# Signs of the input weights on VectorE, a transposed block copy, and redrawn planner priorities in a fused delta-rule and two-layer-pair kernel

## The chip, the cores and the metric

The kernel runs on one core of one Trainium2 chip. The metric is device time in microseconds; the median of three runs of the kernel before is 1029.02 us (1028.18 to 1032.16). In the profile PE is TensorE's matmuls, PEld its weight loads, DVE VectorE, ACT ScalarE, POOL GpSimd and SP the engine whose queue issues the DMAs.

## The reference

Three steps follow each other. The first is a delta-rule recurrence over 768 steps for 4 batches and 8 heads of width 48; its output, reshaped to 3072 tokens of 384 features, goes through two layer pairs with 2048 hidden features each.

```python
for t in range(S):
    kt, vt, bt = (k_n[:, :, t], v[:, :, t], beta[:, :, t, None])
    y[:, :, t] = np.einsum('bhd,bhde->bhe', q[:, :, t], state)
    v_old = np.einsum('bhde,bhd->bhe', state, kt)
    state = state + bt[:, :, :, None] * np.einsum('bhd,bhe->bhde', kt, vt - v_old)
...
h = x @ w_in;  g = np.where(h > 0, h, np.exp(np.minimum(h, 0)) - 1);  x = g @ w_out
...
h = x @ w_in
P = a[0] + a[1] * h + a[2] * h**2 + a[3] * h**3
Q = 1.0 + np.abs(b[0]) * np.abs(h) + np.abs(b[1]) * h**2
out = (P / (Q + 1e-06)) @ w_out
```

The weights of the layer pairs are double precision and reach the kernel as pairs of 32-bit words.

## The kernel before, in words

**Recurrence.** The 768 steps are cut into 12 chunks of 64, and two chunks make a window (six windows). For each window the Gram products of `g_in` (tiles `gp`, `gd`) are turned into small triangular systems, 32 to a partition, and `t_pieces` (lines 792 to 876) inverts their unit triangular matrices in tile `tt`: seven `row` steps for blocks of 8, eight for blocks of 16, then the off-diagonal block by two products, `px` (four steps: `tt` by `am` into `xx_t`) and `pt` (four steps: `xx_t` by the lower right block of `tt` into `tt`), and `post`, which scales a block and transposes all into `tp_t`. Each step is one product and one sum over the last axis on DVE (`step`, line 833). Then `chain` (line 901) runs each chunk: `ks`, a solve in three parts (`cb`), `yy`, `ku`, which renews the state `s_bd`, and `xx`, the transposition into `xs`. Chunks depend on each other through `s_bd`.

**Layer pairs.** All matrix products of the layer pairs are done in three passes with operands split into a high and a low part (`xh` and `xl`, `gh` and `gl`, two halves of `wi` and of `wor` or `wo`). One block of 9 matmuls of 512 columns makes a hidden tile (`h`) or adds a hidden tile to the output (`o`). The first pair runs window by window, 16 hidden tiles each, with the recurrence of the next window between its blocks. The second pair runs afterwards, 48 steps of 18 and 18 matmuls.

**Weight conversion.** A double-precision word pair becomes a float in `conv_x`, `conv_d` and `conv_s` (lines 657 to 697), in halves of 192 columns: two ACT passes scale the high and the low word; DVE joins them by a shift and an or; then the sign has to be put in. For the second pair (`i2`, `o2`) a second DVE operation takes it from the high word by an and with the top bit. For the first pair (`i1`, `o1`) ACT computes the sign of the high word and POOL multiplies. The first pair's input weights, `i1`, are 16 tiles of two halves, 32 conversions; they pass through tile `ce` and are split into `wi` by an ACT copy and a POOL subtraction. Most of their raw words lie in a part of `wo1` (tile name `wo`) that is free at that time.

**Order.** No engine's order is written by hand. Every operation is recorded with its costs, and `order` (line 311) simulates the machine for eight rounds: an engine takes, of what is ready, the operation with the earliest latest start (`late`), TensorE the group with the smallest number; `backward` (line 530) works out new latest starts from the round before, less a random amount of up to `jit` ns. The best round's order is issued. `SLACK` (line 308) holds its margins, among them the time by which a wide group counts as ready late (`F`). In the head, where TensorE would idle, `gaps` (line 338) puts in filler matmuls (`fill`), as many as the planned idle time holds.

The six windows' `tt` lie in one buffer, `ce` in two; SP issues loads of raw words a few conversions ahead, from within `conv_d`.

Of the kernel before, what the change touches and what calls it, by code (L numbers as in the profile page):

```python
# [10 lines left out]
F32 = mybir.dt.float32  # L11
# [3 lines left out]
AF = mybir.ActivationFunctionType  # L15
# [147 lines left out]


class Op:
    __slots__ = ("n", "eng", "emit", "deps", "succ", "pitch", "lat", "group", "key", "start", "late", "off", "left", "ready", "bytes", "tag", "port")


class Group:
    __slots__ = ("kind", "ops", "n")  # L170


class Recorder:
# [133 lines left out]
SIZE = {"F": 9, "yy": 16, "yt": 48}  # L307
SLACK = {"small": 0, "F": 0, "x": 0, "issue": 500, "rate": 240, "land": 2000, "wait": 1500, "space": 3900, "room": 290, "first": 432, "hold": 400, "jit": 500, "seed": 52809305}


def order(ops, rounds):
    groups = []
    for o in ops:
        if o.group is not None and o.group.ops[0] is o:
            o.group.n = o.n
            groups.append(o.group)
            t = 0
            for m in o.group.ops:
                m.off = t
                t += m.pitch  # L320
        o.late = o.n
    mine = {o: None for o in ops}
    for o in ops:
        o.deps = {d: k for d, k in o.deps.items() if d in mine}
        for d in o.deps:
            d.succ.append(o)
    best = None
    for _ in range(rounds):
        end = simulate(ops)
        if best is None or end < best[0]:  # L330
            best = end, {o: o.start for o in ops}
        backward(ops, end)
    for o, s in best[1].items():
        o.start = s
    return best[0], sorted(ops, key=lambda o: (o.start, o.n))
# [23 lines left out]
def simulate(ops):  # L359
# [96 lines left out]
    while done < total:  # L456
        pick = None
        for e in free:
            if pend[e] or head[e]:
                t = free[e] if head[e] else max(free[e], pend[e][0][0])  # L460
                if pick is None or t < pick[0]:
                    pick = t, e
        t, e = pick
        while pend[e] and pend[e][0][0] <= t:
            _, n, u = heapq.heappop(pend[e])
            head[e].append((u.n if e == "PE" else u.late, n, u))
        if e == "PE":
            small = [x for x in head[e] if x[2].kind != "F"] if mode not in (None, "F") else None
            x = min(small or head[e])
            if x[2].kind != "F" and SLACK["hold"] and stall(x[2], t) > SLACK["hold"]:  # L470
                wide = [y for y in head[e] if y[2].kind == "F"]
                if wide:
                    x = min(wide)
            head[e].remove(x)
            u = x[2]
            if mode is not None:
                stop = began + pe_cost(mode, u.kind) * size
                t = max(t, stop)
                if u.kind == "F":
                    fill = False  # L480
                clock(began, t if fill else stop, t)
                if fill and t > max(stop, 20000) + 500:
                    count += 4 * int((t - max(stop, 20000) - 300) / 430)
                    while count > SLACK["first"] - SLACK["room"] + 254.6 * len(usable):
                        asked = max(t - 3000, asked + SLACK["space"])
                        usable.append(asked + 2450)
                    while count > SLACK["first"] + 254.6 * used[0]:
                        used[0] += 1
            mode, began = u.kind, t
            k = 2.0 if slow else 1.0  # L490
            size = k * len(u.ops) / SIZE[mode] if mode in SIZE else k
            issue(u, t, k)
            began = t = t + shift
            free[e] = t + (u.ops[-1].off + u.ops[-1].pitch) * .95 * k
            for o in u.ops:
                finish(o, o.start + o.lat + 70 * (k - 1))
        else:
            o = choose(e, t)
            if o is None:
                free[e] = pend[e][0][0]  # L500
                continue
            o.start = t
            if e == "SP":
                if len(landed) >= 8:
                    t = o.start = max(t, landed[-8])
                free[e] = t + o.pitch
                bus = max(bus, t + 300) + o.bytes / SLACK["rate"]
                landed.append(max(t + o.lat, bus + SLACK["land"]))
                finish(o, landed[-1])
            else:  # L510
                if o.port:
                    t += max(0.0, port - t - 135)
                    port = t + o.lat
                free[e] = t + o.pitch
                finish(o, t + o.lat)
        done += 1
# [1 line left out]


def backward(ops, end):  # L520
    nxt, seed = end, SLACK["seed"]
    for o in sorted(ops, key=lambda o: (-o.start, -o.n)):
        late = end - o.lat
        for s in o.succ:
            if s.deps[o] == "e" and not o.eng == s.eng == "PE":
                late = min(late, s.late - o.lat - (0 if o.eng == "PE" else 33 if s.eng != "POOL" or s.eng == o.eng else 75))
        if o.eng == "PE":
            late = nxt = min(late, nxt - o.pitch)
        elif o.eng == "SP":
            late -= 900  # L530
        if SLACK["jit"]:
            seed = (seed * 1103515245 + 12345) % 2147483648
            late -= SLACK["jit"] * (seed / 2147483648.0)
        o.late = late


@with_exitstack
def kernel(
# [56 lines left out]
    def sq32(t):  # L595
        return t[:, 0:1024].rearrange("p (a b) -> p a b", b=32)
# [2 lines left out]
        return t.rearrange("p (d x) -> p d x", d=32 // n)[:, :, 0:32 * n].rearrange("p d (a b) -> p d a b", b=32)  # L599

    am, tt = sq32(am_f), sq32(tt_f)
    tp_t = ap1.tile([128, 32, 32], F32, name="tp_t")
    lo_d = {}
    p_d = {}
# [58 lines left out]
    def conv_d():  # L663
        key = k, i, h = conv_q[n_conv[2]]
        n_conv[2] += 1
        t = raw_t.pop(key)
        if k == "o1":
            e = wo1[:, i, HD * h:HD * h + HD]
        else:
            e = conv_t[key] = mp.tile([128, HD], F32, tag="ce", name="ce", bufs=2)  # L670
        hw, lw = t[:, :, 1], t[:, :, 0]
        d = e.bitcast(I32)
        v = vector
        if k[1] == "2":
            v.scalar_tensor_tensor(out=lw, in0=hw, scalar=3, in1=lw, op0=ALU.logical_shift_left, op1=ALU.bitwise_or)
            v.scalar_tensor_tensor(out=d, in0=hw, scalar=-0x80000000, in1=lw, op0=ALU.bitwise_and, op1=ALU.bitwise_or)
        else:
            v.scalar_tensor_tensor(out=d, in0=hw, scalar=3, in1=lw, op0=ALU.logical_shift_left, op1=ALU.bitwise_or)
            act(out=hw.bitcast(F32), in_=hw.bitcast(F32), func=AF.Sign)
        if k[1] == "1":  # L680
            gpsimd.tensor_tensor(out=e, in0=e, in1=hw.bitcast(F32), op=ALU.mult)
        conv_ahead()

# [108 lines left out]
    def t_pieces(w):  # L792
# [58 lines left out]
        def row(n, k, c):  # L851
            a, t = diag(am_f, n), diag(tt_f, n)
            return step(99, t[:, :, 0:c, 0:k], a[:, :, k, 0:k].unsqueeze(2).to_broadcast([128, 32 // n, c, k]), t[:, :, 0:c, k])

        def px(g):
            c0, n = 4 * g, 16 - 4 * g
            c4 = slice(c0, c0 + 4)
            return step(
                7 - g, tt[:, c4, c0:16].unsqueeze(2).to_broadcast([128, 4, 16, n]),
                am[:, 16:32, c0:16].unsqueeze(1).to_broadcast([128, 4, 16, n]), xx_t[:, c4])  # L860

        def pt(g):
            n = 4 * g + 4
            i4 = slice(16 + 4 * g, 20 + 4 * g)
            return step(
                3 - g, xx_t[:, :, 0:n].unsqueeze(2).to_broadcast([128, 16, 4, n]),
                tt[:, 16:16 + n, i4].rearrange("p k i -> p i k").unsqueeze(1).to_broadcast([128, 16, 4, n]), tt[:, 0:16, i4])

        def post():
            t22 = tt[:, 16:32, 16:32]  # L870
# [2 lines left out]
            vector.transpose(  # L873
                out=tp_t.rearrange("p i u -> p (i u)"), in_=tt.rearrange("p c i -> p i c"))

        return [pre1, pre2] + [row(8, k, k) for k in range(1, 8)] + [row(16, k, 8) for k in range(8, 16)] + [px(g) for g in range(4)] + [pt(g) for g in range(4)] + [post]

    wt = {}

# [432 lines left out]
    def t_at(w, t0, t1, t2, t3):  # L1312
        tp = t_pieces(w)
        at(t0, tp[0])
        at(t0 + .3, tp[1])
        el = [4 * k * k for k in range(1, 8)] + [16 * k for k in range(8, 16)] + [1024, 768, 512, 256] + [256, 512, 768, 1024]
        spread(t1, t2, tp[2:-1], [.4 + .0021 * n for n in el])
        at(t3, tp[-1])

# [16 lines left out]
    for i in range(4 * NF):  # L1336
        n = Q["npre"]
# [169 lines left out]
```

## Time and profile before

| | |
|---|---|
| median of three runs | 1029.02 us |
| the profiled execution | 1028.83 us, span 1027.1 us |
| PE busy | 1006.6 us, 98% of the span |
| DVE busy | 888.0 us, 86% |
| ACT busy | 749.4 us, 73% |
| POOL busy | 412.0 us, 40% |
| mean granted clock | 0.994 of full speed |
| chain that ended last, by engine | PE 81%, DVE 8%, ACT 6%, issue 2%, POOL 2% |

A busy PE is counted with modelled ends, so its 98% is not 98% of the peak. The line numbers of most instructions are those of the recorder's `emit` (L191), so tiles tell them apart: `tmp` and `tt` are the inverse, `ce` and `wo` with 128x192 elements the conversion, `wo` with 128x1024 elements the second layer pair. The first wide matmul starts at 93.43 us; up to there only the recurrence and filler run on TensorE.

### The profile page before, as it was taken

What the parts mean: (1) busy time and instruction counts of PE and PEld (TensorE: products, weight loads), DVE (VectorE), ACT (ScalarE), POOL (GpSimd) and SP (SyncE); (2) the same over time, 40 slices, a digit from 0 to 9 for tenths busy, and PEclk for the clock granted to TensorE, in tenths of its full rate; (3) what the DMA queues carried; (4) which work ended last, traced back from release to release, by engine and by line L of the source; (5) the groups of instructions that cost most, each with busy time, mean ns of one, the idle gap of its engine ahead of it and who ended that gap; (6) DMA issues with size and microseconds to landing.
All of it is one profiled execution on the core that took longest, in us unless ns stands there. A gap on an engine that the chain in (4) does not pass through costs nothing.

```text
span 1027.1 us, 23269 instructions
## 1 busy us (share of the span) xinstructions
PE 1006.6 (98%) x9246; PEld 835.0 (81%) x9246; DVE 888.0 (86%) x1282; ACT 749.4 (73%) x1493; POOL 412.0 (40%) x319
## 2 busy tenths in 40 slices
PE   8989999999999999999999999999999999999997
PEld 7867788788888888888888788888888888888885
DVE  4998978996998799779976677999999999999996
ACT  4578799867877777777678788667676766866763
POOL 1475366553332133214222224354463554543332
PEclk9999999999999999999999999999999999999998
DMA  9745165317532642453063883101010010000000
GB/s 271 206 135 180 34 187 172 106 31 217 184 100 75 207 138 79 133 153 124 19 195 120 294 303 123 62 1 62 1 62 1 1 62 1 29 3 1 31 1 31
DMA packets 66956, 106.07 MB, mean 103 GB/s; under 512 B 7840, under 2 KB 40736, under 8 KB 66848
## 3 DMA queue, kind: packets, MB, share of 16 engines
q1 hardware_dynamic: 66848, 104.59, 32.5%
q8 instruction: 72, 1.18, 0.5%
q14 instruction: 36, 0.29, 0.1%
HBM read 82.55 MB, written 22.02 MB: 102 GB/s over the span
## 4 chain that ended last, share of the span: by engine, by line
PE 81%; DVE 8%; ACT 6%; issue 2%; POOL 2%; DMA 1%; SPq 0%; ACTq 0%; POOLq 0%; DVEq 0%
PE o L191 34%; PE h L191 16%; PE h_b L191 10%; PE h_a L191 8%; PE gp L191 3%; PE cb L191 3%; PE y L191 2%; ACT wo L191 2%; DVE wo L191 2%; DVE tmp L191 2%; PE ku L191 1%; PE ks L191 1%; DVE tt L191 1%; ACT e L191 1%; PE h_c L191 1%
## 5 line engine op out<-in xcount | busy, mean ns | idle before, releaser
L191 POOL TENSOR_TENSOR wor<-wo,wor 128x384 fp32r<-128x384 f32 x96 | 124.7, 1301 | 268.9 <-ACT wor L191 260.8
L191 POOL TENSOR_TENSOR gl<-wo 128x1024 fp32r<-128x1024 f32 x47 | 135.2, 2877 | 192.8 <-DVE wo L191 161.3
L191 PE MATMUL o<-gh,wor 128*128 128x512 f32 x576 | 195.1, 396 | 0.0
L191 ACT ACTIVATE wo<-wo 128x1024 f32<-128x1024 f32 (+3 forms) x254 | 152.5, 634 | 48.8 <-DVE wo L191 40.0
L191 PE MATMUL h<-xh,wi 128*128 128x512 f32 x546 | 184.0, 395 | 0.0
L191 PE MATMUL o<-gh,wo 128*128 128x512 f32 x576 | 139.5, 391 | 0.0
L191 PEld LDWEIGHTS o<-gh,wo 128*128 128x128 f32 x576 | 109.0, 189 | 22.8
L191 PEld LDWEIGHTS o<-gh,wor 128*128 128x128 f32 x576 | 108.1, 188 | 22.9
L191 PEld LDWEIGHTS h<-xh,wi 128*128 128x128 f32 x546 | 102.5, 188 | 22.4 <-ACT e L191 0.2
L191 PE MATMUL o<-gl,wor 128*128 128x512 f32 x288 | 112.8, 392 | 3.4 <-DVE gl L191 3.4
L191 PE MATMUL h<-xl,wi 128*128 128x512 f32 x273 | 106.6, 390 | 0.0
L191 DVE SCALAR_TENSOR_TENSOR e<-e,pe 128x512 f32<-128x512 f32 x96 | 76.7, 800 | 28.9 <-ACT e L191 25.5
L191 PE MATMUL h_b<-xh,wi 128*128 128x512 f32 x300 | 96.4, 389 | 0.0
L191 DVE TENSOR_TENSOR gl<-e,gh 128x512 fp32r<-128x512 f32 x88 | 70.5, 802 | 24.6 <-ACT gh L191 24.5
L191 DVE SCALAR_TENSOR_TENSOR wo<-wo 128x1024 f32<-128x1024 f32 (+2 forms) x71 | 76.7, 1081 | 16.4 <-ACT wo L191 16.3
L191 PE MATMUL h_a<-xh,wi 128*128 128x512 f32 x276 | 88.9, 389 | 0.0
L191 ACT ACTIVATE e<-h 128x512 f32<-128x512 f32 x91 | 54.4, 598 | 36.6 <-PE h L191 30.9
L191 PE MATMUL o<-gl,wo 128*128 128x512 f32 x288 | 74.1, 392 | 2.1 <-DVE gl L191 2.0
L191 ACT ACTIVATE wo<-h_b,ab_sb 128x1024 f32<-128x1024 f32 (+1 forms) x52 | 57.1, 1128 | 23.0 <-PE h_b L191 22.8
L191 ACT ACTIVATE gh<-e 128x512 fp32r<-128x512 f32 x96 | 60.4, 629 | 16.5 <-DVE e L191 8.3
L191 DVE SCALAR_TENSOR_TENSOR gh<-wo,ab_sb 128x1024 fp32r<-128x1024 f32 (+1 forms) x49 | 63.7, 1299 | 6.6 <-ACT wo L191 1.1
L191 ACT ACTIVATE wo<-h_a,ab_sb 128x1024 f32<-128x1024 f32 x46 | 52.3, 1161 | 20.0 <-PE h_a L191 15.6
(127 smaller groups left out, 2157.5 us busy)
## 6 DMA issues: line engine op xcount, KB each, us to landing
gin<-g_in SPq DMA_DIRECT2D x69, 192.0 KB, 4.0
kq<-c_kq SPq DMA_DIRECT2D x22, 512.0 KB, 5.0
kv<-c_kv SPq DMA_DIRECT2D x24, 384.0 KB, 5.8
raw<-w_out SPq DMA_DIRECT2D x42, 192.0 KB, 3.1
raw<-w_in SPq DMA_DIRECT2D x34, 192.0 KB, 3.4
o2d<-cs SPq DMA_DIRECT2D x32, 192.0 KB, 3.5
i2d<-cs SPq DMA_DIRECT2D x32, 192.0 KB, 3.0
wi<-i2d SPq DMA_DIRECT2D x16, 384.0 KB, 3.7
```

What stands on the lines that cost most here:

```text
L191: fn(**{k: v.real() if isinstance(v, View) else v for k, v in kw.items()})
```

## The change

Three edits. In `conv_d` the conversions of `i1` get their sign as those of the second pair do: a second DVE operation in place of the ACT sign pass and the POOL product; `o1` stays as it was. A new step `turn`, behind the last `row` step and ahead of the first `px`, copies the lower right 16x16 block of `tt` with its axes exchanged into a new tile `tc_t` on ACT, and `pt` reads `tc_t` along its rows instead of `tt` across them. In the planner the random amounts are drawn by the operation's number from a mixture of seeds (`draw`, `mixed`, `MIX`) instead of in a running sequence, TensorE's groups other than the wide ones get a rank that is shifted by such a draw, and margins are altered.

```diff
--- before.py
+++ after.py
@@ -163,11 +163,11 @@
 
 
 class Op:
-    __slots__ = ("n", "eng", "emit", "deps", "succ", "pitch", "lat", "group", "key", "start", "late", "off", "left", "ready", "bytes", "tag", "port")
+    __slots__ = ("n", "eng", "emit", "deps", "succ", "pitch", "lat", "group", "key", "start", "late", "off", "left", "ready", "bytes", "tag", "port", "tie")
 
 
 class Group:
-    __slots__ = ("kind", "ops", "n")
+    __slots__ = ("kind", "ops", "n", "rank")
 
 
 class Recorder:
@@ -305,7 +305,25 @@
     ("F", "ku"): 2230, ("F", "yt"): 2266, ("ks", "ks"): 704, ("yy", "yy"): 1371, ("yy", "ku"): 1371, ("yy", "xx"): 1421, ("yy", "gp"): 1435,
     ("ku", "ku"): 755, ("ku", "yy"): 755, ("xx", "ku"): 450, ("xx", "ks"): 477, ("yt", "yt"): 1365}
 SIZE = {"F": 9, "yy": 16, "yt": 48}
-SLACK = {"small": 0, "F": 0, "x": 0, "issue": 500, "rate": 240, "land": 2000, "wait": 1500, "space": 3900, "room": 290, "first": 432, "hold": 400, "jit": 500, "seed": 52809305}
+SLACK = {"small": 0, "F": 200, "x": 30, "issue": 500, "rate": 240, "land": 2300, "wait": 1500, "space": 3900, "room": 290, "first": 432, "hold": 200, "jit": 800, "pj": 40}
+MIX = [
+    (97143513, 1), (80976384, 3), (2505799, 200), (79334811, 200), (73314090, 200), (46793208, 200),
+    (69792616, 200), (68619154, 200), (27185215, 200), (40519137, 200), (78123636, 200), (916308, 200),
+]
+
+
+def draw(seed, n):
+    x = (n * 2654435761 + seed * 40503) & 0xFFFFFFFF
+    x = ((x ^ x >> 15) * 2246822519) & 0xFFFFFFFF
+    x = ((x ^ x >> 13) * 3266489917) & 0xFFFFFFFF
+    return (x ^ x >> 16) / 4294967296.0
+
+
+def mixed(n):
+    for seed, share in MIX[:0:-1]:
+        if draw(seed + 1, n) * share < 1.0:
+            return draw(seed, n)
+    return draw(MIX[0][0], n)
 
 
 def order(ops, rounds):
@@ -313,12 +331,13 @@
     for o in ops:
         if o.group is not None and o.group.ops[0] is o:
             o.group.n = o.n
+            o.group.rank = o.n + (0 if o.group.kind == "F" else SLACK["pj"] * (mixed(o.n) - .5))
             groups.append(o.group)
             t = 0
             for m in o.group.ops:
                 m.off = t
                 t += m.pitch
-        o.late = o.n
+        o.late, o.tie = o.n, mixed(o.n)
     mine = {o: None for o in ops}
     for o in ops:
         o.deps = {d: k for d, k in o.deps.items() if d in mine}
@@ -463,7 +482,7 @@
         t, e = pick
         while pend[e] and pend[e][0][0] <= t:
             _, n, u = heapq.heappop(pend[e])
-            head[e].append((u.n if e == "PE" else u.late, n, u))
+            head[e].append((u.rank if e == "PE" else u.late, n, u))
         if e == "PE":
             small = [x for x in head[e] if x[2].kind != "F"] if mode not in (None, "F") else None
             x = min(small or head[e])
@@ -518,7 +537,7 @@
 
 
 def backward(ops, end):
-    nxt, seed = end, SLACK["seed"]
+    nxt = end
     for o in sorted(ops, key=lambda o: (-o.start, -o.n)):
         late = end - o.lat
         for s in o.succ:
@@ -528,10 +547,7 @@
             late = nxt = min(late, nxt - o.pitch)
         elif o.eng == "SP":
             late -= 900
-        if SLACK["jit"]:
-            seed = (seed * 1103515245 + 12345) % 2147483648
-            late -= SLACK["jit"] * (seed / 2147483648.0)
-        o.late = late
+        o.late = late - SLACK["jit"] * o.tie
 
 
 @with_exitstack
@@ -599,6 +615,7 @@
         return t.rearrange("p (d x) -> p d x", d=32 // n)[:, :, 0:32 * n].rearrange("p d (a b) -> p d a b", b=32)
 
     am, tt = sq32(am_f), sq32(tt_f)
+    tc_t = ap1.tile([128, 16, 16], F32, name="tc_t")
     tp_t = ap1.tile([128, 32, 32], F32, name="tp_t")
     lo_d = {}
     p_d = {}
@@ -671,13 +688,13 @@
         hw, lw = t[:, :, 1], t[:, :, 0]
         d = e.bitcast(I32)
         v = vector
-        if k[1] == "2":
+        if k[1] == "2" or k in ('i1',):
             v.scalar_tensor_tensor(out=lw, in0=hw, scalar=3, in1=lw, op0=ALU.logical_shift_left, op1=ALU.bitwise_or)
             v.scalar_tensor_tensor(out=d, in0=hw, scalar=-0x80000000, in1=lw, op0=ALU.bitwise_and, op1=ALU.bitwise_or)
         else:
             v.scalar_tensor_tensor(out=d, in0=hw, scalar=3, in1=lw, op0=ALU.logical_shift_left, op1=ALU.bitwise_or)
             act(out=hw.bitcast(F32), in_=hw.bitcast(F32), func=AF.Sign)
-        if k[1] == "1":
+        if k[1] == "1" and k not in ('i1',):
             gpsimd.tensor_tensor(out=e, in0=e, in1=hw.bitcast(F32), op=ALU.mult)
         conv_ahead()
 
@@ -859,12 +876,15 @@
                 7 - g, tt[:, c4, c0:16].unsqueeze(2).to_broadcast([128, 4, 16, n]),
                 am[:, 16:32, c0:16].unsqueeze(1).to_broadcast([128, 4, 16, n]), xx_t[:, c4])
 
+        def turn():
+            act(out=tc_t, in_=tt[:, 16:32, 16:32].rearrange("p k i -> p i k"), func=AF.Copy)
+
         def pt(g):
             n = 4 * g + 4
             i4 = slice(16 + 4 * g, 20 + 4 * g)
             return step(
                 3 - g, xx_t[:, :, 0:n].unsqueeze(2).to_broadcast([128, 16, 4, n]),
-                tt[:, 16:16 + n, i4].rearrange("p k i -> p i k").unsqueeze(1).to_broadcast([128, 16, 4, n]), tt[:, 0:16, i4])
+                tc_t[:, 4 * g:4 * g + 4, 0:n].unsqueeze(1).to_broadcast([128, 16, 4, n]), tt[:, 0:16, i4])
 
         def post():
             t22 = tt[:, 16:32, 16:32]
@@ -873,7 +893,7 @@
             vector.transpose(
                 out=tp_t.rearrange("p i u -> p (i u)"), in_=tt.rearrange("p c i -> p i c"))
 
-        return [pre1, pre2] + [row(8, k, k) for k in range(1, 8)] + [row(16, k, 8) for k in range(8, 16)] + [px(g) for g in range(4)] + [pt(g) for g in range(4)] + [post]
+        return [pre1, pre2] + [row(8, k, k) for k in range(1, 8)] + [row(16, k, 8) for k in range(8, 16)] + [turn] + [px(g) for g in range(4)] + [pt(g) for g in range(4)] + [post]
 
     wt = {}
 
@@ -1313,7 +1333,7 @@
         tp = t_pieces(w)
         at(t0, tp[0])
         at(t0 + .3, tp[1])
-        el = [4 * k * k for k in range(1, 8)] + [16 * k for k in range(8, 16)] + [1024, 768, 512, 256] + [256, 512, 768, 1024]
+        el = [4 * k * k for k in range(1, 8)] + [16 * k for k in range(8, 16)] + [0, 1024, 768, 512, 256] + [256, 512, 768, 1024]
         spread(t1, t2, tp[2:-1], [.4 + .0021 * n for n in el])
         at(t3, tp[-1])
```

## Rows read from the trace of the kernel before

**Rows 1.** stretches: us, busy us (instructions) of PE PEld DVE ACT POOL, clock, DMA, GB/s

```profile
35.50:60.35 24.85, 21.91 (x102) 18.98 (x101) 24.19 (x32) 16.28 (x58) 17.00 (x21) 1.00 0.44 123
60.35:93.43 33.08, 31.59 (x912) 25.31 (x912) 28.14 (x80) 28.19 (x89) 21.48 (x35) 0.90 0.61 181
...
187.00:620.00 433.00, 431.22 (x5181) 357.84 (x5182) 360.15 (x664) 330.00 (x771) 132.75 (x109) 1.00 0.46 145
...
100.00:120.00 20.00, 18.63 (x86) 14.96 (x84) 20.00 (x27) 17.08 (x39) 8.96 (x9) 1.00 0.16 50
...
80.00:82.00 2.00, 1.91 (x21) 1.20 (x13) 1.47 (x4) 2.00 (x8) 1.84 (x5) 0.50 0.66 181
```

**Rows 2.** the chain that ended last, in order of time: start us, us, what

```profile
264.82 2.27 PE h L191 x9
...
289.64 4.08 PE h L191 x18
```

**Rows 3.** waits of PE from 93.4 us: us in total, times, longest us

```profile
PE o L191 <- DVE gl L191: 5.4, 5, 2.0
PE h_c L191 <- ACT pe L191: 1.2, 1, 1.2
PE xt L191 <- ACT y L191: 0.4, 1, 0.4
```

**Rows 4.** the page, part 5, one group of matmuls

```profile
L191 PE MATMUL o<-gl,wor 128*128 128x512 f32 x288 | 112.8, 392 | 3.4 <-DVE gl L191 3.4
```

**Rows 5.** the timeline of DVE from 35 to 61 us: start, us, tiles, idle before

```profile
35.50 1.23 DVE L191 TENSOR_TENSOR tmp<-tt,am 128x1024 f32<-128x1024 f32 x1
...
38.16 0.95 DVE L191 TENSOR_TENSOR tmp<-tt,am 128x768 f32<-128x768 f32 x1
39.03 0.76 DVE L191 SCALAR_TENSOR_TENSOR ce<-wo 128x192 int32<-128x192 int32 x1
...
41.33 0.68 DVE L191 TENSOR_TENSOR tmp<-tt,am 128x512 f32<-128x512 f32 x1
...
43.17 0.41 DVE L191 TENSOR_TENSOR tmp<-tt,am 128x256 f32<-128x256 f32 x1
...
45.90 0.57 DVE L191 TENSOR_TENSOR tmp<-xx_t,tt 128x256 f32<-128x256 f32 x1
46.38 0.35 DVE L191 SCALAR_TENSOR_TENSOR ce<-wo 128x192 int32<-128x192 int32 x1
46.65 0.41 DVE L191 TENSOR_REDUCE tt<-tmp 128x64 f32<-128x256 f32 x1
...
47.24 1.08 DVE L191 TENSOR_TENSOR tmp<-xx_t,tt 128x512 f32<-128x512 f32 x1
...
49.22 1.78 DVE L191 TENSOR_TENSOR tmp<-xx_t,tt 128x768 f32<-128x768 f32 x1
51.50 0.74 DVE L191 SCALAR_TENSOR_TENSOR ce<-wo 128x192 int32<-128x192 int32 x1 [0.50 <-POOL wi L191]
...
53.03 0.53 DVE L191 SCALAR_TENSOR_TENSOR ce<-wo 128x192 int32<-128x192 int32 x1
53.48 1.95 DVE L191 TENSOR_TENSOR tmp<-xx_t,tt 128x1024 f32<-128x1024 f32 x1
```

**Rows 6.** groups by line and form from 35.5 to 93.4 us

```profile
L191 ACT ACTIVATE wo<-wo 128x192 f32<-128x192 f32 x61 | 21.1, 375 | 6.1 <-DVE ce L191 5.5 <-DVE wo L191 0.3
...
L191 DVE SCALAR_TENSOR_TENSOR ce<-wo 128x192 int32<-128x192 int32 x18 | 9.1, 509 | 0.5 <-POOL wi L191 0.5
```

**Rows 7.** the timeline of ACT from 37 us

```profile
38.28 1.20 ACT L191 ACTIVATE wo<-wo 128x192 f32<-128x192 f32 x4 [3.80 <-DVE ce L191]
```

**Rows 8.** the timeline of POOL from 37 us

```profile
38.75 0.83 POOL L191 TENSOR_TENSOR ce<-ce,wo 128x192 f32<-128x192 f32 x1 [10.26 <-ACT wo L191]
```

**Rows 9.** the timeline of PE from 80 us

```profile
80.30 3.44 PE L1421 MATMUL fill<-cm_sb 128*128 128x256 f32 x8
```

**Rows 10.** the timeline of DVE from 76 us

```profile
80.48 1.12 DVE L191 TENSOR_TENSOR R<-R,cb 64x384 f32<-64x384 f32 x2 [1.09 <-PE cb L191]
```

## The prediction

> **What bounds the kernel now.** I read the stretches first [rows 1]. From 187 to 620 us TensorE is busy 431.2 of 433.0 us, so there the kernel is as long as its matmul stream. The wide matmuls alone (3456 of 512 columns by the code: 6 windows x 288 and 48 pairs x 36) take 4.08 us for 18, 0.227 us each [rows 2], so 783 us, and only fewer interruptions could shorten the rest: a block of 9 that a small group follows takes 2.27 us instead of 2.04 [rows 2]. Next the waits of TensorE from its first wide matmul at 93.4 us on [rows 3]: 5.4 us for DVE's `gl`, 1.2 us for `pe`, 0.4 us for `y`. Of the 5.4 us, 3.4 us belong to `wor`, the first layer pair [rows 4]; the other 2.0 us are the last product's, in the tail. All that a better order can recover behind 93.4 us is therefore some 5 us, and a little at the interruptions. What is left is the head: the wide stream starts when the first window has run through its serial steps. From 35.5 to 60.35 us DVE is busy 24.19 of 24.85 us [rows 1], which is the end of the block inverse with weight conversion between its steps. From 60.35 to 93.43 us the two chunks run through TensorE, ACT and DVE in turn; DVE and ACT are busy 28.1 and 28.2 of 33.1 us, and the granted clock falls to 0.90. So DVE sets the head's first part, hand-offs its second.
>
> **Part 1, the transposed copy.** Each window has four `pt` products that read `tt` with the two block axes exchanged. In window 0 the 256, 512, 768 and 1024 elements take 0.57, 1.08, 1.78 and 1.95 us, and the four `px` products of the same sizes, read along the row, 0.41, 0.68, 0.95 and 1.23 us [rows 5]. Sums 5.38 and 3.27: reading `tc_t` along its rows should save 2.1 us of DVE where DVE has no idle time. Bounds: 0 (if `xx_t`'s broadcast were what is slow; but `px` broadcasts an operand in the same way) and -2.6 (DVE's wait of 0.50 us at 51.50, right behind the slow 768 product, goes too). I take -2.1, the difference of like rows.
>
> The added ACT copy of 256 elements has no row; a 128x192 one takes 0.375 us [rows 6], so it lies between that and 0.50 (the same, scaled to 256); about 0.4. In window 0 it comes free at 35.5 us, and ACT is idle for 3.80 us before 38.28 us [rows 7]; its reader starts at 45.90, so it costs nothing; without that cover it would cost its own 0.4 to 0.5 us. It does add a wait: the first `pt` waits on ACT, and behind that on DVE's in-order queue stand `gl` and `e`, which the wide stream needs. In each window the four `px` steps lie between copy and reader, 8.6 us in window 0 (35.50 to the end of the last one's sum), so I count 0. In windows 1 to 5 the saving recurs (some 2 us each), but TensorE idles 1.8 us in 433 there: worth nothing by itself.
>
> **Part 2, the sign of the input weights.** 32 conversions each lose an ACT pass (0.37 us) and a POOL product (0.83 us in [rows 8]) and gain a second DVE operation like the one that stays. That one lasts 0.35 us and lets the next start 0.27 us later (46.38 to 46.65, [rows 5]). 18 of the 32 are done before 93.4 us [rows 6]: 9 starting before 60.09 us, 9 from there on.
>
> In the first part the second operation adds 9 x 0.27 = 2.4 us to the full engine. Against it stands what POOL's product costs DVE: at 39.03 us the same operation lasts 0.76 us, 0.41 more, while POOL has run the product since 38.75 [rows 5, 8]; the five DVE instructions that so meet a `ce` product, from 39.03 to 53.03, last 1.5 us longer together (0.41, 0.39, 0.25, 0.30, 0.18). At 51.50 it is POOL's subtraction for `wi` that DVE waits for (0.50 us) and meets (0.74 us), and that stays. So +2.4 - 1.5 = +0.9. Bounds: -2.4 (the planner puts all nine behind 60.35 us, and the hold-up at 51.50 of 0.50 + 0.39 goes with the 1.5) and +6.1 (each new operation is held up for 0.41 us as well and nothing is relieved). I take +0.9, which goes by the rows where DVE met that product, and keeps the hold-ups by the subtraction. Both parts together: the first solve 1.2 us earlier, near 59 us.
>
> By the Trainium skill, SBUF — State Buffer, section "Who interferes with whom", a DVE instruction with two SBUF inputs and a GpSimd instruction that reads SBUF exclude each other, the later one blocking whole. The trace agrees (0.76 beside 0.35 us), and the rule speaks against the change as well as for it: the new operation has two SBUF inputs like the old. The sum by it alone would be the +6.1 above; it is the rival on the slower side.
>
> In the second part DVE gets 2.4 us more, in 4.9 us of idle; ACT loses 9 x 0.37 = 3.4 us and POOL nine products. These I set against each other: 0, with bounds of -1.5 (four ACT passes of 0.375 us, [rows 6], fewer ahead of the chain's own ACT steps) and +4.9 (14 hand-offs on DVE or ACT, each late by one more 0.35 us operation).
>
> **Part 3, the redrawn order.** Draws now belong to an instruction's number, last over all rounds, reach 800 instead of 500 ns, and move TensorE's small groups by up to 20 places; wide groups count as ready 200 ns later. No row prices it; I go by what it can recover. (a) At 80.30 us eight filler matmuls run until 83.7 us at a granted clock of 0.50 (of the two levels, 1.2 GHz), while their successor's operand `R` was ready at 81.60 [rows 1, 9, 10]: 2.0 us of the chain stand behind filler. Filler counts come from planned idle time, so a new plan draws them anew: -2.0 to +2.0, I take half the loss, -1.0. (b) The 3.4 us for `gl` [rows 4] stand where DVE has no gap (20.00 of 20 us from 100 us on, [rows 1]); 200 ns of caution and a shorter queue should take more than half: -2.0, bounds -3.4 and +3. (c) The other waits -0.4; and of 61 changes from wide to small work (counted along TensorE's timeline to 620 us, 0.23 us each by [rows 2]) four or five fewer: -1.0, bounds +-2.3.
>
> **Sum.** -1.2 - 1.0 - 2.0 - 1.4 = -5.6 us. The profiled execution took 1028.83 us (span 1027.1), 0.2 us under the median of 1029.02, so 1023.2 us.
>
> **Rivals.**
> 1. Only the head gains: part 3 loses elsewhere what it wins, because TensorE's order is at its floor (1.8 us idle of 433). -1.2 and perhaps the filler's 1.0: 1026.6 to 1027.6 us. For it: the floor. Against: 3.4 us of `gl` waits sit in one layer pair.
> 2. The parts don't do what they say: the product stays slow, or the conversion moves into the gained time: 1028 to 1031 us. For it: DVE is full in the head, and the planner fills gaps.
> 3. Slower: the lock. Place: DVE's queue from 35.5 to 93.4 us. Price: 18 operations of 0.27 + 0.41 = 12.2 us, less 2.1 and 1.5, less 2.5 of the second part's idle time, = +6.1: 1034.9 us. It decides as soon as the first solve starts after 61 us in spite of the faster products. For it: POOL still runs a subtraction per conversion. Against: POOL loses half of its instructions there.
> 4. A larger gain: all filler loss, all 5.0 us of waits before the tail and twice the switches go: -1.2 - 2.0 - 5.0 - 2.0 = -10.2: 1018.6 us.
>
> **How the numbers follow.** This kernel's measurement can tell 0.5%, 5.1 us, from no change, so the forecast lies just past the line. Chances: forecast 0.36 (its own range 1020 to 1023.9), rival 1 0.27, rival 2 0.12, rival 3 0.13, rival 4 0.12. Faster by over 0.5%: 0.36 + 0.12 = 0.48; within 0.5%: 0.27 + 0.12 = 0.39; slower: 0.13. The range takes in rivals 1, 2 and 4 with their bounds and stops short of rival 3: 1014.5 to 1031 us.
>
> **What would show it.** The `tmp` product from `xx_t` and `tc_t` at 1.2 us for 1024 elements; 32 POOL products and 32 ACT passes gone; the first solve near 59 us and the first wide matmul near 91; DVE conversion operations seldom over 0.5 us; TensorE's waits for `gl` under 3.5 us in all; the stretch from 620 to 1006 us unchanged. Wrong if the first wide matmul comes after 93.4 us, or if waits of another name of over 5 us stand behind it.

## The result and the profile after

The changed kernel takes 1017.82 us (median of 4 runs, 1016.61 to 1019.66) against 1029.16 us: ratio 0.9886, 95% interval 0.9861 to 0.9912. The forecast was 1023.2, so the time fell by twice what was forecast. The profiled execution took 1017.70 us with a span of 1015.9 us; the gain of 11.2 us of span can be read at two points of time:

| | before | after | difference | forecast |
|---|---|---|---|---|
| first solve starts | 60.35 us | 57.13 us | -3.2 | -1.2 |
| from there to the first wide matmul | 33.1 us | 30.8 us | -2.3 | -1.0 |
| from the first wide matmul to the end | 933.7 us | 928.0 us | -5.7 | -3.4 |
| waits of TensorE in that last part, all | 7.0 us | 2.4 us | -4.6 | -2.4 |

The stretches of the changed kernel, in the columns of [rows 1] (length, then busy time and instructions of PE, PEld, DVE, ACT and POOL, granted clock):

```profile
35.50:57.13 21.63, 20.16 (x94) 17.43 (x93) 21.59 (x43) 13.02 (x46) 5.71 (x8) 1.00 0.42 112
57.13:87.92 30.79, 29.68 (x850) 24.04 (x850) 28.77 (x84) 25.27 (x75) 16.43 (x25) 0.94 0.64 197
87.92:181.00 93.08, 92.75 (x1316) 76.63 (x1309) 84.77 (x165) 84.54 (x229) 49.79 (x56) 1.00 0.49 145
181.00:614.00 433.00, 432.76 (x5073) 360.16 (x5072) 351.07 (x667) 337.48 (x785) 130.61 (x113) 1.00 0.46 148
```

In the first part of the head DVE is still without idle time (21.59 of 21.63 us), but the part is 3.2 us shorter, and POOL, 17.0 us busy there in [rows 1], is down to 5.7. From 181 to 614 us TensorE idles 0.2 us of 433, where it idled 1.8.

DVE's timeline in the head shows the products, and conversion operations between the steps:

```profile
38.55 0.35 DVE L191 SCALAR_TENSOR_TENSOR wo<-wo 128x192 int32<-128x192 int32 x1
38.82 0.95 DVE L191 TENSOR_TENSOR tmp<-tt,am 128x768 f32<-128x768 f32 x1
39.69 0.35 DVE L191 SCALAR_TENSOR_TENSOR ce<-wo 128x192 int32<-128x192 int32 x1
39.95 0.95 DVE L191 TENSOR_REDUCE xx_t<-tmp 128x64 f32<-128x768 f32 x1
...
45.85 0.39 DVE L191 TENSOR_TENSOR tmp<-xx_t,tc_t 128x256 f32<-128x256 f32 x1
...
47.11 0.69 DVE L191 TENSOR_TENSOR tmp<-xx_t,tc_t 128x512 f32<-128x512 f32 x1
...
49.04 0.96 DVE L191 TENSOR_TENSOR tmp<-xx_t,tc_t 128x768 f32<-128x768 f32 x1
...
51.94 1.21 DVE L191 TENSOR_TENSOR tmp<-xx_t,tc_t 128x1024 f32<-128x1024 f32 x1
```

The four products that read `tc_t` take 0.39, 0.69, 0.96 and 1.21 us, 3.25 in all, where [rows 5] had 5.38. The conversion operations at 38.55 and 39.69 last 0.35 us each and start the next instruction 0.27 us later; the one at 39.03 of [rows 5] lasted 0.76. Over the whole head the groups that answer to [rows 6] are these (mean ns behind the busy time):

```profile
L191 ACT ACTIVATE wo<-wo 128x192 f32<-128x192 f32 x40 | 14.5, 381 | 0.9 <-DMA wo<-w_in 0.5 <-DMA wo<-w_out 0.3
...
L191 DVE SCALAR_TENSOR_TENSOR wo<-wo 128x192 int32<-128x192 int32 x26 | 10.2, 392 | 0.0
L191 DVE SCALAR_TENSOR_TENSOR ce<-wo 128x192 int32<-128x192 int32 x16 | 7.0, 436 | 0.0
```

ACT has 40 of the 61 passes of this form. DVE's conversion operations last 0.39 and 0.44 us on the mean; the `ce` ones lasted 0.51 in [rows 6]. The copy on ACT is longer than I had put it:

```profile
36.01 0.65 ACT L191 ACTIVATE tc_t<-tt 128x256 f32<-128x256 f32 x1 [3.29 <-DVE tt L191]
```

It takes 0.65 us and stands behind 3.29 us of idle time, ten microseconds ahead of its reader. Of the eight filler matmuls of [rows 9] four are left, and they end when the operand is ready and not 2.0 us behind it. Each is shorter, too: 0.28 us at a granted clock of 1.00 from 77.2 to 78.4 us, where the eight took 0.43 each at a mean of 0.63 from 80.3 to 83.7. The timelines of PE and of DVE:

```profile
77.24 1.13 PE L1441 MATMUL fill<-cm_sb 128*128 128x256 f32 x4
78.30 1.44 PE L191 MATMUL cb<-R,tp_t 32*32 32x48 f32 x64
```

```profile
77.42 1.14 DVE L191 TENSOR_TENSOR R<-R,cb 64x384 f32<-64x384 f32 x2 [0.30 <-PE cb L191]
```

The waits of TensorE from the first wide matmul on, which answer to [rows 3]:

```profile
PE o L191 <- DVE gl L191: 2.0, 1, 2.0
PE h L191 <- issue: 0.2, 1, 0.2
PE h L191 <- DVE xl L191: 0.2, 1, 0.2
```

What is left is the 2.0 us of the last product in the tail. The 3.4 us of [rows 4] and the 1.2 us for `pe` are gone.

### The profile page after: what moved, and what is told of

The parts are those of the page before. It is cut to its first block, busy times and chain, and to the rows that moved or that the text cites. A ratio compares the mean times of both kernels' runs of the same rounds, so it can differ in the third digit from the quotient of the medians.

```text
span 1015.9 us, 23204 instructions
## 1 busy us (share of the span) xinstructions
PE 1001.9 (99%) x9234; PEld 833.6 (82%) x9234; DVE 870.4 (86%) x1314; ACT 746.4 (73%) x1467; POOL 388.3 (38%) x287
## 4 chain that ended last, share of the span: by engine, by line
PE 88%; DVE 4%; DMA 3%; ACT 3%; issue 1%; SPq 0%; DVEq 0%; ACTq 0%
PE o L191 37%; PE h L191 18%; PE h_b L191 10%; PE h_a L191 9%; PE cb L191 3%; PE gp L191 3%; PE y L191 2%; PE ku L191 2%; PE ks L191 1%; DMA gin<-g_in 1%; ACT wo L191 1%; PE h_c L191 1%; DMA xg<-g_in 1%; PE xt L191 1%; DVE wo L191 1%; DVE tmp L191 1%
## 5 line engine op out<-in xcount | busy, mean ns | idle before, releaser
L191 POOL TENSOR_TENSOR wor<-wo,wor 128x384 fp32r<-128x384 f32 x96 | 115.6, 1207 | 269.5 <-ACT wor L191 256.7
L191 POOL TENSOR_TENSOR gl<-wo 128x1024 fp32r<-128x1024 f32 x47 | 141.1, 3002 | 191.4 <-DVE wo L191 155.4
L191 ACT ACTIVATE wo<-wo 128x1024 f32<-128x1024 f32 (+3 forms) x224 | 143.0, 671 | 37.2 <-DVE wo L191 34.1
L191 DVE SCALAR_TENSOR_TENSOR wo<-wo 128x192 int32<-128x192 int32 (+2 forms) x101 | 88.0, 875 | 16.2 <-ACT wo L191 16.1
L191 DVE TENSOR_TENSOR gl<-e,gh 128x512 fp32r<-128x512 f32 x88 | 73.6, 836 | 18.7 <-ACT gh L191 18.4
L191 ACT ACTIVATE e<-h 128x512 f32<-128x512 f32 x91 | 54.4, 598 | 35.5 <-PE h L191 33.9
L191 PEld LDWEIGHTS h_b<-xh,wi 128*128 128x128 f32 x300 | 56.3, 188 | 11.7
```

Source lines behind the costliest of these rows:

```text
L191: fn(**{k: v.real() if isinstance(v, View) else v for k, v in kw.items()})
```

## The experiments

Theory P says that the two parts carry the gain, theory R that the redrawn order does, theory F that the draws happen to fit. Each run is compared with the kernel before in the same session. "Behind" is the span from the first wide matmul on, "waits" what TensorE waits for in it. The four columns of times are of each run's profiled execution, which lies up to 2.4 us off the median of its executions; the ratios go by the medians.

| run | ratio (95%) | first solve | first wide | behind | waits |
|---|---|---|---|---|---|
| before | 1 | 60.35 | 93.43 | 933.7 | 7.0 |
| changed kernel | 0.9886 (0.9861 to 0.9912) | 57.13 | 87.92 | 928.0 | 2.4 |
| copy, order kept | 0.9981 (0.9969 to 0.9992) | 58.19 | 90.80 | 932.0 | 6.0 |
| sign, order kept | 1.0041 (1.0026 to 1.0055) | 64.22 | 96.91 | 932.8 | 7.5 |
| both, order kept | 1.0035 (1.0020 to 1.0049) | 62.26 | 95.92 | 935.9 | 8.1 |
| sign, order kept, pair apart | 0.9987 (0.9970 to 1.0003) | 59.76 | 92.85 | 932.2 | 6.5 |
| new planner, neither part | 1.0059 (1.0042 to 1.0076) | 63.09 | 96.62 | 937.2 | 9.9 |
| old planner, both parts | 0.9925 (0.9905 to 0.9946) | 56.78 | 88.53 | 929.4 | 4.6 |
| fresh seed 1, both parts | 0.9941 (0.9924 to 0.9958) | 56.56 | 87.97 | 931.3 | 5.8 |
| fresh seed 2, both parts | 0.9911 (0.9890 to 0.9931) | 56.47 | 89.11 | 928.5 | 3.0 |
| fresh seed 3, both parts | 0.9961 (0.9947 to 0.9974) | 58.46 | 92.23 | 931.6 | 6.5 |
| seed 2, neither part | 1.0096 (1.0076 to 1.0116) | 61.80 | 93.49 | 942.1 | 10.4 |
| seed 2, sign alone | 0.9963 (0.9948 to 0.9978) | 58.53 | 91.87 | 930.0 | 5.4 |
| seed 2, copy alone | 0.9963 (0.9948 to 0.9977) | 59.23 | 90.30 | 932.9 | 6.2 |

### Order kept: the parts without a new plan

The planner records the work of before and orders it as before; only when an instruction is issued another one takes its place.

**The copy alone.**

```diff
         def emit():
-            fn(**{k: v.real() if isinstance(v, View) else v for k, v in kw.items()})
+            if sub is not None:
+                sub()          # the product, reading the copy
+            else:
+                fn(**{k: v.real() if isinstance(v, View) else v for k, v in kw.items()})
...
             o.emit()
+            if o.hook is not None:
+                o.hook()       # the copy, behind the last row step's sum
```

> Before's order of instructions is kept one for one; only the copy on ACT is added behind the last row step, and the four products of each window read it. Theory P (the parts carry the gain): the first solve comes 2.0 to 2.2 us earlier than before's 60.35 us, the first wide matmul as much earlier than 93.43, and the time is 2 us lower (1027). Theory R (the redrawn order carries it): DVE's gain is caught by a later wait, and the time stays within 1 us of before's 1029.2.

1025.71 us against 1028.01. The timeline of PE, first solve and first wide matmul:

```profile
58.19 1.36 PE L195 MATMUL cb<-kv,tp_t 32*32 32x48 f32 x64 [0.40 <-POOL ce L195]
...
90.80 0.50 PE L195 MATMUL h<-xh,wi 128*128 128x512 f32 x1
```

The first solve comes 2.16 us earlier, the first wide matmul 2.63 us, and the median is 2.3 us lower: theory P. How the 2.16 come about is less simple than the forecast. The products take 0.39, 0.69, 1.20 and 1.21 us here, 1.89 less than in [rows 5], and DVE's wait of 0.50 us at 51.50 is gone; two short operations behind them last some 0.3 us longer. The third product still overlaps a POOL subtraction:

```profile
49.03 1.20 DVE L860 TENSOR_TENSOR tmp<-xx_t,tc_t 128x768 f32<-128x768 f32 x1
```

**The sign alone.**

```diff
+            def two():
+                h_, l_, d_ = hw.real(), lw.real(), d.real()
+                nc.vector.scalar_tensor_tensor(out=l_, in0=h_, scalar=3, in1=l_, ...)
+                nc.vector.scalar_tensor_tensor(out=d_, in0=h_, scalar=-0x80000000, in1=l_, ...)
+            if now:                    # an input-weight conversion, i1
+                rc.sub = two           # issued in the place of the next line
             v.scalar_tensor_tensor(out=d, in0=hw, scalar=3, in1=lw, ...)
+            if now:
+                rc.sub = lambda: None  # nothing in the place of the ACT pass
             act(out=hw.bitcast(F32), in_=hw.bitcast(F32), func=AF.Sign)
...
+            rc.sub = (lambda: None) if now else None
             gpsimd.tensor_tensor(out=e, in0=e, in1=hw.bitcast(F32), op=ALU.mult)
```

> Before's order is kept; only the sign of the 32 input-weight conversions is put in by a second DVE operation right behind the first, and the ACT pass and the POOL product are gone. Theory P: POOL meets DVE less, the conversion operations fall from a mean of 0.51 us towards 0.35, the first solve comes 0 to 1.5 us earlier, the second half of the head 1 to 2 us shorter for lack of ACT passes before the chain's own: 1026 to 1028. Theory R: the 2.4 us that the new operations add ahead of the first solve eat the relief: 1028.5 to 1031. The lock rival: each new operation is held up by POOL's subtraction, the first solve comes after 61 us: 1033 or more.

1032.10 us, the first solve 3.9 us later: slower, which neither P nor R expected so far, and near the number of the lock rival. DVE's timeline, with one pair that POOL doesn't touch and then one that it does:

```profile
43.79 0.35 DVE L686 SCALAR_TENSOR_TENSOR wo<-wo 128x192 int32<-128x192 int32 x1
44.25 0.36 DVE L687 SCALAR_TENSOR_TENSOR ce<-wo 128x192 int32<-128x192 int32 x1
44.52 0.42 DVE L195 TENSOR_TENSOR tmp<-tt,am 128x256 f32<-128x256 f32 x1
...
60.31 0.74 DVE L686 SCALAR_TENSOR_TENSOR wo<-wo 128x192 int32<-128x192 int32 x1
61.16 0.96 DVE L687 SCALAR_TENSOR_TENSOR ce<-wo 128x192 int32<-128x192 int32 x1
```

In the pair at 43.79 both operations last some 0.35 us. The second starts 0.46 us after the first, whose result it reads, and the next, which doesn't read its result, 0.27 us after the second. The nine pairs ahead of the first solve start 0.39 to 0.46 us apart (hold-ups taken off), 1.5 us more in all than nine times 0.27. In the pair at 60.31 the operations last 0.74 and 0.96 us, and POOL runs the subtractions that split a weight from 59.97 to 61.90:

```profile
59.97 0.87 POOL L195 TENSOR_TENSOR wi<-ce,wi 128x192 fp32r<-128x192 f32 x1
60.85 1.05 POOL L195 TENSOR_TENSOR wor<-wo,wor 128x384 fp32r<-128x384 f32 x1
```

Eight of the conversion operations ahead of the first solve are held up in this way, 3.0 us in all over 0.35 each; in the kernel before it was 2.4 us. So the bare cost is 2.4 (nine more operations), 1.5 (the wait within the pair) and 0.6 (hold-ups): 4.5 us for the 3.9 measured. Against it stand DVE's wait of 0.50 us at 51.50, which is gone, and the 768-element product, which takes 1.53 us instead of 1.78.

**Both.** The two edits above together.

> Before's order is kept, with both parts in it. Theory P: the sum of the two alone, first solve near 57.4 us (where the filler before it ends) to 58.5, 1023.5 to 1025.5. Theory R: 1028 to 1030, and the whole gain of 11.3 us is the new order's.

1031.18 us; the first solve lies 1.96 us ahead of the sign alone, nearly the copy's 2.16. The time is above both ranges, R's by 1.2 us: without a new plan the two parts lose. Even so R does not follow, as the runs with a new plan show. In the profiled execution, 2.3 us over the median, the span behind the first wide matmul is 3.9 us longer than with the copy alone. TensorE waits 2.1 us more there (8.1 against 6.0), and the granted clock falls to 0.83 from 190 to 200 us, which costs some 1.7 us, an estimate (0.17 of 10 us):

```profile
190.00:200.00 10.00, 9.95 (x157) 7.84 (x158) 7.65 (x19) 4.52 (x11) 4.50 (x4) 0.83 0.16 45
```

**The sign alone, with the pair apart.** As the run with the sign alone, with the second operation in the place of POOL's product:

```diff
+            rc.sub = two_b if now else None    # two_b: the second operation, two: the first alone
             gpsimd.tensor_tensor(out=e, in0=e, in1=hw.bitcast(F32), op=ALU.mult)
```

> Before's order with the sign on DVE as in the run that kept the order, but the second operation stands where POOL's product stood in the order, so that in most cases another DVE instruction lies between it and the first. If what made the kept order slow is that the second operation waits for the first (a pair starts the next work 0.66 to 0.73 us after its own start there, where one operation takes 0.27), the first solve comes at 61 to 62.5 us instead of 64.22 and the time is 1028.5 to 1030. If it is POOL's subtraction that holds each operation up (the lock), the place changes nothing: 63.5 to 65 us and 1031 to 1033.

1026.96 us, 5.1 us under the run with the pair together, and the first solve at 59.76, earlier than expected of either. Against the kernel before, the interval takes in 1: no difference is shown. DVE's timeline, with `ce` operations that now stand away from their partner, and one that is held up:

```profile
39.26 0.35 DVE L690 SCALAR_TENSOR_TENSOR ce<-wo 128x192 int32<-128x192 int32 x1
39.53 0.35 DVE L686 SCALAR_TENSOR_TENSOR wo<-wo 128x192 int32<-128x192 int32 x1
39.80 0.94 DVE L195 TENSOR_REDUCE xx_t<-tmp 128x64 f32<-128x768 f32 x1
40.66 0.35 DVE L690 SCALAR_TENSOR_TENSOR ce<-wo 128x192 int32<-128x192 int32 x1
40.93 0.35 DVE L686 SCALAR_TENSOR_TENSOR wo<-wo 128x192 int32<-128x192 int32 x1
41.20 0.68 DVE L195 TENSOR_TENSOR tmp<-tt,am 128x512 f32<-128x512 f32 x1
...
51.36 0.78 DVE L686 SCALAR_TENSOR_TENSOR wo<-wo 128x192 int32<-128x192 int32 x1
```

Within each group of these operations a start lies 0.26 or 0.27 us behind the one before it. The wait within the pair is gone, and of the hold-ups two are left ahead of the first solve, 0.5 us in all. These two differences, 1.5 and 2.5 us, are 4.0 of the 4.46 us between the two runs' first solves; one conversion operation fewer stands ahead of it, 0.3 us more. So the lock has no fixed price: the same operations meet POOL eight times in one place and twice in another, with POOL's subtraction in both. Against the kernel before, eight operations more (2.2 us) and 1.9 us less of hold-ups make +0.3. DVE's wait of 0.50 us at 51.50 is gone, and the 768-element product takes 1.54 us instead of 1.78: -0.4 in all, for -0.6 measured.

### The plan alone

After's planner with before's work:

```diff
-        if k[1] == "2" or k in ('i1',):
+        if k[1] == "2":
...
-        if k[1] == "1" and k not in ('i1',):
+        if k[1] == "1":
...
-                tc_t[:, 4 * g:4 * g + 4, 0:n].unsqueeze(1).to_broadcast([128, 16, 4, n]), tt[:, 0:16, i4])
+                tt[:, 16:16 + n, i4].rearrange("p k i -> p i k").unsqueeze(1).to_broadcast([128, 16, 4, n]), tt[:, 0:16, i4])
...
-        return [...] + [turn] + [px(g) for g in range(4)] + ...
+        return [...] + [px(g) for g in range(4)] + ...
```

> The changed planner (draws, margins) with the work of before: sign of the input weights by ACT and POOL, products across the block, no copy. Theory P: the plan alone gives what it recovers in waits behind the first wide matmul, at most 4 to 5 us: 1024 to 1029. Theory R: 1019 to 1021. If the draws fit only the work for which they were chosen (theory F), the plan alone is no better than before: 1028 to 1033.

1034.38 us: above every range given. The new planner recovers nothing by itself: 9.9 us of waits, more than before's 7.0. Theory R falls, as far as one order can show it: a draw goes by an operation's number, and numbers shift where operations come or go, so with other work the same seeds are another draw.

### New plans for both parts

**Old planner, both parts.** Before's kernel with the edits to `conv_d` and `t_pieces` of the change and nothing else; before's seed and margins.

> Both parts are in the work and the planner of before, with its seed and margins, makes a new order for it (the random sequence falls on other operations than before). Theory P (the parts, planned for, carry the gain): first wide matmul at 89 to 91 us, 1020 to 1024. Theory F (the changed draws are a lucky fit to this very work): first wide matmul at 91 to 96, 1024 to 1033.

1020.59 us, first wide matmul at 88.53: P. Three quarters of a per cent come without the change's planner.

**Three fresh seeds.** The changed kernel with one seed for all draws:

```diff
-MIX = [
-    (97143513, 1), (80976384, 3), (2505799, 200), ...
-]
+MIX = [(1234567, 1)]      # then 31415926, then 27182818
```

> The changed kernel, its margins and both parts, with one fresh seed for all draws instead of the mixture. Theory P: 1016 to 1022, the first wide matmul at 87 to 90 us. Theory F: 1022 to 1032, the first wide matmul at 90 to 95 us, and waits of TensorE behind it of 2 to 8 us where the changed kernel has 1.

1022.29 us, the first wide matmul at 87.97 as under P, but waits of 5.8 us as under F.

> As the first fresh seed, with another: theory P 1016 to 1022, theory F 1022 to 1032. Two fresh seeds further apart than 4 us speak for F in any case: the order then weighs as much as either part.

1019.06 us: P, with little between it and the changed kernel.

> A third fresh seed: theory P 1016 to 1022, theory F 1022 to 1032. Under F the time goes with the start of the first wide matmul, 928 to 936 us of span behind it in every run.

1024.22 us: F. The seeds lie 5.2 us apart, more than either part was worth or cost with the order kept (2.3 and 4.1 us).

### Two by two with one seed

The second seed's kernel without the sign edit, without the copy, and without both; the edits are those shown for the plan alone. The seed is the same, but its draws fall on other operations in each of the four (see the plan alone). So they are four draws, and a difference of up to 0.75%, which the draws make among the kernels with both parts, can be the draw's.

> The changed planner with the second of the fresh seeds, for the work of before (neither part). It starts a two by two with that seed, whose run with both parts took 1019.1. Theory P (the parts carry the gain once the order is planned for them): 1027 to 1034, first solve 60 to 63 us. Theory F (fit by luck): within 3 us of 1022.

1038.51 us, more than any range had. The waits of TensorE behind the first wide matmul are spread over the chain's steps, and only the 2.0 us for `gl` are the tail's as in every run (us in total, times, longest):

```profile
PE cb L191 <- DVE R L191: 2.1, 4, 0.9
PE gp L191 <- ACT xs L191: 2.1, 1, 2.1
PE o L191 <- DVE gl L191: 2.0, 1, 2.0
PE cb L191 <- ACT R L191: 1.9, 3, 1.1
PE o L191 <- POOL gl L191: 1.3, 1, 1.3
```

They cost more than their own time. The stretches from the first wide matmul to 300 us, of this run whole and three pieces of it, then of the run with both parts and the same seed:

```profile
93.49:300.00 206.51, 197.93 (x2477) 165.88 (x2470) 172.44 (x319) 162.89 (x421) 98.32 (x100) 0.97 0.43 133
```

```profile
160.00:170.00 10.00, 7.83 (x274) 6.29 (x264) 7.36 (x14) 9.18 (x30) 5.13 (x7) 0.86 0.42 124
170.00:180.00 10.00, 10.00 (x148) 8.22 (x148) 4.28 (x9) 7.93 (x24) 5.68 (x8) 0.80 0.40 117
...
280.00:300.00 20.00, 15.98 (x347) 13.93 (x348) 18.54 (x60) 12.96 (x36) 2.17 (x3) 0.83 0.75 237
```

```profile
89.11:300.00 210.89, 210.47 (x2683) 175.66 (x2679) 184.49 (x356) 174.75 (x444) 90.94 (x94) 1.00 0.43 133
```

TensorE is idle 2.2 us of the first piece and 4.0 us of the last, and the granted clock falls to 0.86, 0.80 and 0.83, that is to the lower level of 1.2 GHz for a part of each; with both parts TensorE is busy 210.5 of 210.9 us at full clock. An estimate from these rows: the clock costs 1.4, 2.0 and 3.4 us in the three pieces, 6.8 in all, and the waits are 7.4 us longer than with both parts (10.4 against 3.0); together 14.2, for the 13.6 us by which the span behind the first wide matmul is longer.

> The same planner and seed, with the sign on DVE alone. Theory P: two thirds of what both parts give over none, 1021 to 1026, first solve 57.5 to 59.5 us. Theory T (the copy carries it): within 2 us of the run with neither.

1024.42 us, 14.1 us under neither; both parts give 19.5 (1038.51 - 1019.06). P, with some 0.7 of the gain. The granted clock is 1.00 in every stretch from the first wide matmul to 1000 us.

> The same planner and seed, with the transposed copy alone. Theory P: 2 to 4 us under the run with neither, first solve 58 to 60.5 us. Theory T: nearly all of the gain, 1019 to 1022.

1024.71 us, 13.8 us under neither, where 2 to 4 were expected: a miss. The first solve moves by 2.6 us only; the rest is behind the first wide matmul (942.1 to 932.9 us). The granted clock is 1.00 from the first wide matmul to 1000 us here, too. Either part, in this one draw, takes the plan out of the bad stretches above, so the two don't add up.

## Why the prediction came out as it did

The direction held and the time lies in the range; the size was off by half. Theory P explains it, in a form that I had not put: with the order kept the two parts together cost 0.35%, the new planner without them costs 0.6%, and both parts with a new plan gain in each of five orders. In the head the gain is traced below. Behind the first wide matmul TensorE waits less; why the two parts spare it these waits was argued, not shown. The copy relieves DVE (with seed 2 its busy time falls from 883.0 to 873.2 us). The sign does not (883.6 us alone); what it takes away is ACT's and POOL's work (751.6 to 743.6 and 410.6 to 392.4 us).

- **Part 1, -2.1 us at the first solve:** right, and to the tenth by luck. The 1.78 us of the 768-element product held some 0.25 us of hold-up by POOL (1.53 and 1.54 in the two runs with the sign alone), which the prediction counts a second time, as the 0.30 among part 2's five. From row to row the products alone give 1.86 (5.11 to 3.25 us, sign alone against both with the order kept); the rest of the 2.16 is the wait of 0.50 us at 51.50, put down as a bound, less new hold-ups. The copy's 0.4 us was wrong: 0.65, outside my bounds, since I scaled a row whose words lie next but one, and the copy reads across rows; it was hidden as foreseen. "In windows 1 to 5 worth nothing by itself" stands with the order kept: the median fell by 2.3 us and the first wide matmul came 2.6 us earlier, and the 1.7 us by which the span behind it fell are those of one execution that ran 1.1 us under its median. Under a new plan it did not stand, in the one draw tried: with seed 2 the span behind fell by 9.2 us.
- **Part 2, +0.9 us:** wrong in sign, and the step of the prediction that failed first, in two terms. It counted nine more operations ahead of the first solve (2.4 us), and the new plan put only three more there (0.8). And it kept the hold-ups that POOL's subtraction makes: ahead of the first solve seven of twelve conversion operations of before were held up, by 2.4 us in all (1.2 of it by the subtraction); of the changed kernel's fifteen one, by 0.16 us (0.51 at 40.82). Its bound of -2.4 had both. Taken from start to start on DVE's timeline, the products and the wait of 0.50 us behind one of them take 2.7 us less, the conversion operations 1.6 less, small operations that now stand there 1.3 more, the rest 0.2 less: the -3.2 measured. With seed 2 the sign alone brings the first solve 3.3 us forward, in one draw. The pitch of 0.27 us was right where other work stands between; in a pair it is up to 0.46. The lock (the Trainium skill, SBUF — State Buffer, "Who interferes with whom") is no less real, 0.76 beside 0.35 us in [rows 5]; with POOL busy 5.7 instead of 17.0 us there was less to meet. Rival 3, the lock, did not come about in the changed kernel. With the order kept its condition was met (first solve at 62.26 us with both parts), but the run with the sign alone puts it down to 0.6 us of lock beside 1.5 of waiting within pairs and 2.4 of added work.
- **Part 3 (a), filler, -1.0 us:** right in kind, and all of the 2.0 us were got back, by fewer filler matmuls at a higher granted clock; the second part of the head is 2.3 us shorter.
- **Part 3 (b) and the other waits, -2.4 us:** the size was -4.6, and the reason was wrong. The caution of 200 ns and the draws did not remove them by themselves: the plan alone has more waits (9.9). With one seed they go from 10.4 to 5.4 or 6.2 by one part and to 3.0 by both. But the draw has a share: the five orders with both parts have 2.4 to 6.5 us, and the changed kernel's is the least of them.
- **Part 3 (c), fewer changes from wide to small work, -1.0 us:** failed. 61 became 60. The span behind shrank by 1.1 us beyond the waits. Some 0.6 of them lie behind the first `h_a` matmul (632.58 and 622.00 us), in the second layer pair; the cause was not settled.
- **The rivals:** number 4 named the nearest time, 1018.6, with the filler and the waits gone; its doubled switches did not happen, and a head 2.0 us better than its -1.2 made up for them. That its time was so near is luck in part.

One thing limits what the 1.1% says. Among eight orders, the five with both parts lie from 0.9886 to 0.9961, the three with neither from 1 to 1.0096. The groups don't overlap, but within the first, where four of the five have the same margins, a draw moves the time by 0.75%; within the second the range is 1%, draws and margins together. The kernel before and the changed kernel are each the best of their group. Like for like there are three pairs: with the old planner the parts are worth 0.75% (1 to 0.9925), with the changed one and its mixture of seeds 1.7% (1.0059 to 0.9886), with seed 2 1.85% (1.0096 to 0.9911), where the order with neither is the slowest of all. Which of the margins in `SLACK` matter was not tried.

## What to carry to other kernels

Where an order is planned from costs, price an edit under several draws, and once with the old order kept: the kept order shows the bare cost (here -0.2% for the copy; for the sign +0.4% with its two operations together and none clear of noise with them apart), the draws show what the planner makes of it (-1.3% each, in one draw each, which is too few). When two dependent short DVE operations are added, let the plan put other work between them. And look for what an edit changes behind the stage for which it was made, too: half of this gain lies behind the first wide matmul, where TensorE is busy nearly all the time (431.2 of 433.0 us in [rows 1]), most of it in waits for other engines, and such waits can cost clock as well.

## What the runs showed of the hardware

- Of two DVE operations on 128x192 elements the second starts 0.27 us after the first if it doesn't need its result, 0.39 to 0.46 if it does; both last 0.35 us.
- ACT's copy of 256 elements read across rows took 0.65 us in window 0 and 0.685 us on the mean of six, more than a 128x512 copy in a row at 0.63.
- In the run with seed 2 and neither part TensorE idled 2.2 us from 160 to 170 us and 4.0 us from 280 to 300 us, at granted clocks of 0.86 and 0.83. In the kernel before it idled 2.0 us from 180 to 200 us at 1.00. So idle time in the middle of the matmul stream can cost clock, and does not each time.
